# A recurrent attention block with a gated feed-forward behind it: four early inverses by halves, copies on another engine, and a new written order

## The chip, the core and the metric

The kernel runs on one core of a Trainium2 chip. A core has a matrix engine (TensorE, PE in the profile, with its weight loads as PEld), a vector engine (VectorE, DVE), a scalar engine (ScalarE, ACT), a general engine (GpSimd, POOL) and a queue that only starts transfers (SyncE, SP). Each takes its own instructions in the order in which they are written, and waits where an instruction needs what another has not delivered. Transfers (DMAs) are started by SP, by POOL and, at the very start, by ACT. The metric is the device time of one execution, in microseconds (us).

## The reference

Six arrays of shape 4 x 8 x 768 x 40 (batch, heads, steps, width) go through a recurrence with a 40 x 40 state for each of the 32 sequences:

```python
for t in range(S):
    y[:, :, t] = einsum('bhd,bhde->bhe', rt, state)
    Sa = einsum('bhde,bhe->bhd', state, at)
    state = state * wt[:, :, None, :] - einsum('bhd,bhe->bhde', Sa, bt)
    state = state + einsum('bhd,bhe->bhde', vt, kt)
```

The outputs of the 8 heads are put side by side (3072 tokens of 320 numbers), normalised by their root mean square and scaled by `rms_g`, and go through `silu(x @ w_gate) * (x @ w_val) @ w_out` with 1536 hidden columns. The weights arrive as 64-bit floats, and the kernel itself makes 32-bit floats of them.

## The kernel before

**Chunks.** The 768 steps are cut into 24 chunks of 32. Within a chunk the recurrence is written with products of matrices, which needs the inverse of one 32 x 32 unit triangular matrix for each of the 32 sequences. For chunk `c` there are three stages. `front(c)` loads the chunk and forms decays, keys and the triangular matrices: `LT` holds them, and `where(...)` copies the valid parts of products into `LT` under masks (`near` for steps 1, 2 and 3 apart inside groups of four, `msk` for the longer levels). `inverse(c)` sends `LT` through memory (`sB`) into `M`, where each of the 128 partitions holds a quarter of the rows of one sequence, and eliminates with 31 pairs of VectorE instructions (`tmp <- Yi, M` and `Yi <- Yi, tmp`); the result goes back through memory (`sY`) into `LT`. `main(c)` uses state, inverse and keys for the chunk's outputs: it forms `Xs`, then `U = inverse x Xs`, copies `U` into `VU`, updates the state `ST`, forms the scores `As` under masks `msi`, and sums five levels into `y`; then come the norm and `xg`, the scaled, turned tokens.

**Feeds.** After each pair of chunks `feed(g)` runs the feed-forward on 256 tokens: twelve slices of the hidden columns, each with products into `ps`, a silu on ScalarE (`sg`), a product on VectorE (`hT`), and products into `po`. There are 12 feeds. `narrow_slice(f)` turns the 64-bit weights into 32-bit ones on VectorE and ScalarE and writes them to memory (`sW`); this is spread over the first feed, and every feed loads its slices from `sW`.

**The order.** Nothing is scheduled while the kernel is built. Each stage only records pieces (one instruction, or one group of products), and `ORDER` is a written list that says in which order the recorded pieces are issued; `PAIRS` says which pair of PSUM banks each room uses. A piece's place in the list fixes its place in its engine's queue. A dash in the list issues a dummy product of the identity into an unused corner of `po` (`plan.warm`, line 1002 in the profile). It computes nothing. The numbers in the functions' arguments (`more=`, load names, the tables `PRODUCTS` and `LOADS`) only describe pieces to the plan; with a written list they change no instruction.

The profile gives most instructions the line of a helper: 475 for VectorE, 502, 498 and 505 for ScalarE, 521 and 524 for products, 518 for transfers, 514 for POOL's memsets. So the text goes by the names of tiles.

Of the kernel before, what the change touches and what calls it, by code (L numbers as in the profile page):

```python
# [7 lines left out]
FP32 = mybir.dt.float32  # L8
# [8 lines left out]
P = 128  # L17
# [4 lines left out]
S0, S1 = 15.0, 2.0  # L22
LEAD = 2
WARM = 230.0
# [3 lines left out]
PRODUCTS = {  # L28
    "out": (0.915, 0.359, 0.434, 0, 2560), "h": (1.618, 0.306, 0.381, 0, 4096), "h64": (0.864, 0.2, 0.2, 1, 2048),
    "turn": (0.824, 0.2, 0.273, 0, 2048), "turn3": (0.278, 0.3, 0.275, 0, 768), "turn4": (0.388, 0.249, 0.272, 0, 1024),  # L30
    "turny": (0.46, 0.145, 0.248, 2, 640), "gram": (0.927, 0.124, 0.264, 2, 512), "gramk": (0.927, 0.158, 0.263, 2, 1792),
    "score": (0.927, 0.138, 0.243, 2, 1024), "level": (0.603, 0.132, 0.216, 5, 1024), "state": (0.597, 0.126, 0.245, 3, 640),
    "lower": (0.594, 0.126, 0.216, 4, 320), "update": (0.603, 0.154, 0.265, 2, 1280), "y0": (0.613, 0.132, 0.236, 2, 1024),
}

LOADS = {
    "sB": (1.75, 0.1), "LT": (2.0, 0.2), "M": (2.67, 0.44), "sY": (1.96, 0.3), "wf": (4.02, 1.46), "r": (4.25, 0.69),
    "tok": (2.09, 0.27), "wn": (2.36, 0.31), "wan": (2.68, 0.51), "out": (1.9, 0.15), "g": (2.37, 0.68),
    "raw2": (3.1, 0.75), "raw64": (2.21, 0.27), "rawo": (2.9, 0.7), "rawp": (2.4, 0.3), "sW": (1.5, 0.7),
}  # L40
# [5 lines left out]
36 33 2 26 42 1 31 0 25 343 37 29 107 38 24 36 26 34 262 2 13 1 35 40 0 190 24 339 13 14 - - - 40 17 44 15 41 43 55  # L46
42 8 60 47 175 72 48 45 84 185 59 68 186 585 54 58 - - - - - 49 93 586 53 179 69 71 599 81 176 57 597 50 67 178 609
70 188 80 622 51 92 16 623 65 610 52 56 177 633 64 66 - - - - - - - - - - - - 61 189 9 598 77 79 187 78 587 620 62 0
587 81 - - - - 72 75 179 82 62 90 595 384 194 588 87 11 633 89 589 74 395 620 197 590 380 88 73 195 391 - - - - 101
196 209 390 610 84 102 214 381 201 611 202 5 212 86 213 383 591 85 0 222 92 591 611 17 95 221 224 223 384 94 234 225  # L50
- - 197 233 237 93 391 245 246 592 328 393 198 598 645 612 0 641 598 15 612 592 - 338 205 206 380 642 599 209 0 207
612 200 0 337 612 186 598 6 326 613 2 599 641 34 176 200 216 217 23 600 389 215 33 201 355 95 202 177 96 214 - - - -
211 187 339 93 0 577 0 561 578 297 579 171 192 53 187 191 - - - 182 188 200 623 172 185 625 186 580 562 581 612 355
582 199 1065 197 583 611 183 198 624 184 0 152 1005 850 298 0 298 0 837 295 0 0 0 83 130 298 148 0 298 83 0 507 307
833 0 303 555 0 840 307 0 290 0 67 125 316 314 0 132 125 67 0 0 131 314 0 286 325 0 130 0 298 130 0 291 292 - - - -
- 287 0 293 0 304 0 316 305 301 0 0 283 0 296 0 311 0 322 281 0 286 0 295 280 0 292 - - - - - - - - - - - - - - - -
- 288 0 0 0 0 301 0 285 62 301 116 305 0 283 250 116 0 - - - - - - - - 293 0 258 112 296 0 110 300 256 0 308 307 245
293 292 0 0 304 0 288 0 301 - - - - - - 298 306 0 0 313 0 297 0 0 0 293 310 494 301 0 494 0 302 0 0 299 492 0 0 296
0 246 0 791 0 0 0 787 0 0 93 468 2 796 94 469 0 94 462 794 0 467 93 94 290 461 95 462 96 468 511 97 469 291 98 470
481 289 99 292 471 0 99 100 101 471 102 472 103 481 511 104 482 105 488 106 489 107 483 2 490 108 109 0 293 109 490  # L60
0 108 0 0 379 0 379 387 0 387 369 0 405 378 387 406 0 - - - - - - - - - - - - - - - - - - - - - - - - - - - - - - -
- - - - - - - - - - - - - - - - - - - - - - - - - - - - - - - - - - - - - - - - 44 0 367 377 0 415 0 42 0 414 383 43
412 0 383 410 0 383 40 373 0 0 0 0 0 0 36 0 377 - - - - - - - - - - - - - - - - - 44 0 377 35 44 0 414 0 0 82 0 32 -
43 0 373 0 90 0 229 407 38 88 0 40 78 226 42 38 41 47 48 0 43 226 42 50 45 48 396 0 50 396 43 0 396 0 0 379 395 380
0 395 380 0 401 0 394 0 378 242 400 44 0 400 47 0 145 45 377 242 0 145 391 377 0 216 1 145 391 42 635 398 429 626
146 0 397 39 145 426 634 398 146 147 631 43 623 44 621 45 632 46 148 47 622 - - - - 639 375 376 149 48 416 239 641
830 150 399 377 640 840 0 150 641 653 48 838 151 658 152 645 828 - - - - - - 642 153 670 154 646 155 682 49 656 50
156 669 657 51 157 666 158 667 52 159 643 668 - - - - - - - 53 389 160 161 678 162 1 651 652 - 647 2 702 655 3 654 0
594 610 611 609 625 595 636 109 608 110 596 373 - - - - - - - - - - - 605 590 374 111 345 783 607 626 782 383 112
627 620 622 385 793 113 623 606 375 382 114 792 621 - - - - - - - 617 384 115 376 346 116 377 619 117 635 634 118  # L70
618 378 119 - - - - - 160 633 120 379 121 163 380 161 122 381 123 162 124 164 386 - - - - - - - - - 629 125 387 126
127 128 388 129 630 130 640 631 389 638 131 390 - - - - - 167 641 132 391 133 639 134 392 168 135 393 - - - - - 165
136 394 137 138 430 139 166 571 431 581 643 140 - - - 171 721 644 580 141 642 142 570 143 174 645 144 173 145 178 -
- - 182 175 146 177 147 172 150 149 179 - - - 180 148 637 176 185 732 432 186 433 0 1065 584 283 - 39 1064 36 582 38
284 638 37 40 635 583 0 17 635 480 625 567 497 40 18 624 498 41 284 568 626 42 285 499 627 43 570 286 642 636 44 500
2 706 287 45 643 897 0 493 500 501 643 287 897 656 644 648 2 45 597 907 502 649 494 0 457 860 458 0 613 0 457 611
552 0 - 596 457 621 598 0 622 0 456 595 610 853 457 622 458 634 854 0 505 - - - 500 360 765 521 361 449 531 519 764
504 532 543 362 508 363 0 500 517 543 501 4 515 363 502 364 506 419 514 365 5 366 516 367 0 367 419 368 421 369 370
420 422 44 0 370 - 430 371 44 0 3 40 0 367 426 368 369 370 504 371 37 372 373 374 375 429 376 526 525 521 377 505
522 0 338 466 390 339 397 377 9 340 391 341 392 342 430 393 398 343 480 440 400 378 439 395 387 429 396 394 403 408  # L80
388 0 403 0 342 474 700 403 578 0 700 403 342 709 490 343 0 474 7 696 405 343 709 475 403 344 0 487 706 472 0 485
695 10 343 704 404 0 404 0 4 404 37 405 0 401 31 337 481 402 45 0 474 3 337 338 41 339 402 0 42 3 0 398 705 399 471
50 335 400 898 336 703 470 401 337 37 907 338 339 402 27 480 699 908 704 340 403 341 897 479 486 701 889 343 700 584
478 890 713 714 481 899 702 719 28 706 559 900 342 712 29 560 731 30 0 531 9 0 9 683 684 17 10 0 10 454 0 450 552 10
451 0 10 672 0 672 - - - - - - - - - - - - - - - - 662 25 0 27 670 26 0 682 680 24 695 539 677 676 678 704 661 37 -
- - - 3 36 675 662 296 4 681 434 691 663 679 692 703 672 5 0 0 428 1 680 683 42 682 666 43 687 681 667 20 40 686 21
677 695 2 22 292 0 675 705 287 0 675 287 688 0 671 0 669 665 269 7 17 410 8 682 29 411 412 30 667 413 414 0 8 665 0
675 8 681 672 9 674 0 9 672 - - - - - - - - - - 481 0 9 37 483 411 0 471 0 25 5 401 6 402 403 404 471 7 39 405 473 -
- - - - - - - - - - - 16 0 0 28 8 27 397 0 397 28 0 397 0 654 462 0 5 396 36 8 397 398 37 399 14 47 462 15 0 457 10
723 44 3 11 43 458 583 644 21 12 646 582 4 13 645 461 0 571 21 13 572 458 393 22 14 394 15 466 0 391 455 19 0 372 0  # L90
16 436 0 694 28 5 27 442 6 695 371 439 7 0 696 0 451 370 435 6 760 0 745 0 428 0 741 362 425 0 751 433 362 741 0 748
362 0 425 423 358 733 0 358 0 744 358 432 359 360 0 427 428 0 7 359 0 359 15 0 359 360 6 0 425 0 428 442 359 360 361
362 363 364 0 360 361 742 362 0 362 363 364 419 365 742 366 367 2 368 423 751 369 370 371 372 373 424 675 374 7 0
424 2 0 1154 672 0 1154 421 422 732 432 738 0 669 730 1002 732 670 420 995 731 439 742 685 985 421 0 993 421 687 735
# [160 lines left out]

class Piece:


    def __init__(self, engine, key, issue, time, tail, drain=0.0, mode=-1, area=0, many=0, load=None, since=0.0):
        self.engine, self.key, self.issue = engine, key, issue  # L260
        self.time, self.tail, self.drain, self.mode, self.area = time, tail, drain, mode, area
# [773 lines left out]
```

## Time and profile before

| | |
|---|---|
| median of 3 runs | 1106.53 us (1105.67 to 1109.04) |
| the profiled execution | 1106.7 us, all of it span |
| TensorE busy | 1032.9 us, of which 75.7 in dummy products |
| VectorE busy | 907.4 us |
| ScalarE busy | 453.9 us |
| POOL busy | 302.7 us |
| first `hT` of the first feed | starts at 173.5 us |
| dummy products | from 5.3 to 225.5 us |

The profiled execution's time stands 0.2 us from the median, so its rows can be used against the median as they are. Busy time is the time covered by an engine's instructions. VectorE's and ScalarE's rows overlap: an instruction starts some 0.1 us before the row of the one in front ends, so the sum of a queue's rows is more than its busy time. "us to landing" is the time from the issue of a transfer to its end.

### The profile page before, as it was taken

How to read it: one execution, taken by the hardware profiler on the slowest of the kernel's cores; microseconds unless marked ns; L12 is line 12 of the kernel's file. 1: busy time of each engine (PE TensorE's matmuls, PEld its weight loads, DVE VectorE, ACT ScalarE, POOL GpSimd, SP SyncE). 2: the span in 40 equal slices, each digit the busy share in tenths (PEclk: the TensorE clock that was granted, in tenths of full speed). 3: DMA queues.
4: the chain of work that ended last, by engine and by line, in shares of the span. 5: the costliest groups of instructions: out<-in, count | busy, mean ns of one | idle time of the engine just before them, and what ended most of it. 6: DMA issues, size and time to landing. Idle time of an engine off the chain costs nothing.

```text
span 1106.7 us, 53122 instructions
## 1 busy us (share of the span) xinstructions
PE 1032.9 (93%) x23152; PEld 852.5 (77%) x23152; DVE 907.4 (82%) x3065; ACT 453.9 (41%) x989; POOL 302.7 (27%) x534
## 2 busy tenths in 40 slices
PE   5697888989999999999999999999989999999998
PEld 4597877767778877877777877887878878787876
DVE  5998999799889888798789789988898889798421
ACT  3644544654244344344344345334335435332211
POOL 7520342122233223223323323413404312200000
PEclk9789899989999999999999999999999999999999
DMA  7545453786555536456535545645636546434242
GB/s 158 134 85 164 122 125 85 198 240 165 124 141 124 149 80 160 117 125 141 150 101 138 138 123 134 154 101 151 139 95 166 125 112 147 108 108 131 80 141 80
DMA packets 171177, 145.43 MB, mean 131 GB/s; under 512 B 123712, under 2 KB 142080, under 8 KB 170944
## 3 DMA queue, kind: packets, MB, share of 16 engines
q1 hardware_dynamic: 152576, 119.06, 39.8%
q0 software_dynamic: 16192, 22.64, 11.0%
q8 instruction: 182, 2.98, 1.2%
q10 hardware_dynamic: 2176, 0.33, 0.2%
q14 instruction: 51, 0.42, 0.1%
HBM read 125.83 MB, written 16.12 MB: 128 GB/s over the span
## 4 chain that ended last, share of the span: by engine, by line
PE 59%; DVE 19%; issue 7%; ACT 3%; DMA 3%; POOL 2%; SPq 0%; DVEq 0%; POOLq 0%; ACTq 0%
PE ps L521 41%; PE po L521 11%; PE ps L524 7%; DVE LT L475 3%; DVE tmp L475 3%; DVE Yi L475 2%; DVE As L475 2%; DVE y L475 2%; DVE K L475 1%; DVE hT L475 1%; DVE r L475 1%; DVE ex L475 1%; DVE wf L475 1%; ACT K L502 1%; DMA sB<-LT 1%
## 5 line engine op out<-in xcount | busy, mean ns | idle before, releaser
L521 PE MATMUL ps<-xg,wf 128*128 128x256 f32 (+1 forms) x1728 | 354.5, 392 | 3.1 <-DVE xg L475 2.1
L521 PEld LDWEIGHTS ps<-xg,wf 128*128 128x128 f32 (+1 forms) x1728 | 261.3, 189 | 58.4 <-issue 14.3
L521 PE MATMUL po<-wf,hT 128*128 128x320 f32 x576 | 178.8, 444 | 3.2 <-DVE hT L475 1.8
L475 DVE TENSOR_TENSOR tmp<-Yi,M 128x60 f32<-128x60 f32 (+24 forms) x744 | 156.0, 210 | 18.1 <-DMA M<-sB 1.9
L475 DVE TENSOR_TENSOR Yi<-Yi,tmp 128x60 f32<-128x60 f32 (+24 forms) x744 | 155.3, 209 | 15.9
L518 POOL DMA_DIRECT2D VU<-in_v_dram x92 | 53.4, 587 | 356.6 <-PE ps L524 206.3
L498 ACT ACTIVATE sg<-ps 128x256 f32<-128x256 f32 x144 | 53.7, 383 | 236.4 <-PE ps L521 225.0
L521 PEld LDWEIGHTS po<-wf,hT 128*128 128x128 f32 x576 | 102.2, 190 | 39.3 <-issue 3.7
L475 DVE TENSOR_TENSOR hT<-ps,sg 128x256 f32<-128x256 f32 x144 | 59.3, 419 | 54.7 <-ACT sg L498 53.4
L475 DVE TENSOR_TENSOR K<-K,T 128x512 f32<-128x512 f32 (+1 forms) x192 | 93.4, 495 | 8.7 <-PE ps L521 3.4
L521 PEld LDWEIGHTS ps<-Ab,K 40*64 40x64 f32 x4608 | 76.6, 137 | 30.8 <-issue 9.6
L521 PE MATMUL ps<-Ab,K 40*64 40x56 f32 x4608 | 86.4, 223 | 11.5 <-DVE K L475 3.1
L502 ACT COPY K<-K 128x256 f32<-128x256 f32 (+1 forms) x168 | 71.2, 443 | 61.9 <-PE ps L521 40.6
L475 DVE TENSOR_TENSOR As<-ps,msi 128x256 f32<-128x256 f32 (+1 forms) x192 | 83.2, 481 | 10.6 <-PE ps L521 10.4
L502 ACT COPY KN<-ps 128x640 f32<-128x640 f32 x96 | 66.4, 691 | 53.4 <-PE ps L524 20.7
L521 PEld LDWEIGHTS ps<-As,KN 128*40 128x40 f32 x3072 | 67.2, 125 | 19.5 <-issue 11.7
L521 PE MATMUL ps<-As,KN 128*40 128x32 f32 x3072 | 74.5, 206 | 7.3 <-issue 4.6
L1002 PE MATMUL po<-ident 128*128 128x128 f32 x560 | 75.7, 291 | 5.3 <-ACT po L544 5.3
L1002 PEld LDWEIGHTS po<-ident 128*128 128x128 f32 x560 | 70.4, 203 | 6.7 <-POOL wan L514 5.2
L518 POOL DMA_DIRECT2D kbn<-in_b_dram x92 | 53.6, 586 | 78.5 <-PE ps L521 70.8
L518 POOL DMA_DIRECT2D wn<-in_w_dram x92 | 51.5, 566 | 85.9 <-DVE tmp L475 32.4
L518 POOL DMA_DIRECT2D kbn<-in_k_dram x92 | 53.4, 584 | 75.7 <-PE ps L521 75.0
(124 smaller groups left out, 1529.2 us busy)
## 6 DMA issues: line engine op xcount, KB each, us to landing
wf<-sW SPq DMA_DIRECT2D x144, 480.0 KB, 4.2
M<-sB SPq DMA_DIRECT2D x96, 128.0 KB, 3.9
rn<-in_r_dram SPq DMA_DIRECT2D x24, 160.0 KB, 4.3
sW<-ex SPq DMA_DIRECT2D x16, 240.0 KB, 4.0
out_dram<-o SPq DMA_DIRECT2D x48, 80.0 KB, 3.5
kbn<-in_b_dram POOLq DMA_DIRECT2D x92, 40.0 KB, 3.2
wan<-in_w_dram POOLq DMA_DIRECT2D x46, 80.0 KB, 3.9
wan<-in_a_dram POOLq DMA_DIRECT2D x46, 80.0 KB, 4.3
```

The costliest lines, as they stand in the source:

```text
L475: plan.add("DVE", time + more + each * size(o), 0.087, lambda at: fn(at(o), *m(at)), [o], aps(*args))
L498: scalar(o, [a], lambda at: nc.scalar.activation(at(o), at(a), f, **kw), aps(acc), 0.1 if f in (AF.Square, AF.Relu) else 0.0)
L502: scalar(o, [a], lambda at: nc.scalar.copy(at(o), at(a)), extra=more)
L518: plan.add(by, 0.6 if by == "POOL" else 0.45, 0.0, lambda at: queue.dma_start(out=o, in_=i), [o], [i], load=LOADS[load], since=since)
L521: return o, lhsT, rhs, lambda at: nc.tensor.matmul(at(o), lhsT, rhs, start=start, stop=stop, skip_group_check=True), 4
L524: return o, i, ident, lambda at: nc.tensor.transpose(at(o), i, ident), 2
L1002: plan.warm = lambda: nc.tensor.matmul(po_[:, 0, DM:DM + P], ident, ident, start=False, stop=False, skip_group_check=True)
```

## The change

Four things change, and the written list is a new one.

1. For chunks 0 to 3 the stage `inverse(c)` is replaced by `early_inverse(c)`. It inverts the two 16 x 16 diagonal halves of each sequence's matrix on 64 partitions (15 pairs of VectorE instructions), and gets the off-diagonal 16 x 16 block as a product of three blocks, by two groups of 32 small products with a ScalarE copy behind each. Four tiles (`B`, `Y`, `E`, `A`) are laid over the old `M` tile. The result stays in `E`, and `main(c)` reads it there, not in `LT`.
2. The three `near` copies of each front walk the same elements in another order: the eight groups innermost, not the one to three columns.
3. Copies go from VectorE to ScalarE: two of the four `VU` copies of each chunk, the two `r2` copies of each pair of chunks, the scores of the top level (one VectorE product becomes two scaled copies), and `xg` (one VectorE product becomes three scaled copies).
4. `ORDER` and `PAIRS` are new, with 224 dashes where there were 280. The tables that only described pieces go. In `state` the same products are issued in another sequence.

```diff
+    def early_inverse(c):
+        z = Z[c]
+        plan.stage = "inverse", c
+        LT = z["LT"]
+        B, Y, E, A = halves(z["M"])
+        blank(Y[:, :, 0:HC], 0.0)
+        blank(Y.rearrange("p s t -> p (s t)")[:, 0::C + 1], 1.0)
+        for i in range(HC - 1):
+            n, m = i + 1, HC - 1 - i
+            tmp = tmp_.next()[0:2 * BH, 0:n * m].rearrange("p (s t) -> p s t", s=n)
+            tt(tmp, Y[:, 0:n, i:i + 1].to_broadcast((2 * BH, n, m)), B[:, i:i + 1, i + 1:].to_broadcast((2 * BH, n, m)), MUL)
+            tt(Y[:, 0:n, i + 1:HC], Y[:, 0:n, i + 1:HC], tmp, SUB)
+        scale(Y[0:BH, :, HC:], Y[0:BH, :, 0:HC].rearrange("p s t -> p t s"), -1.0)
+        sY = sY_.next()[:, 0:3 * HC * HC].rearrange("n (s t) -> n s t", s=HC)
+        dma(sY[:, :, 0:C], Y[0:BH])
+        dma(sY[:, :, C:], Y[BH:2 * BH, :, 0:HC])
+        blank(E[:, :, 0:HC], 0.0)
+        for i, q in each_iq:
+            dma(E[top(i, 1 - q)], sY[seq(i, q)].rearrange("m s t -> s m t"))
+        ps = plan.room()
+        pe("inv", [mm(ps[...], LT[...], E[..., HC:C]) for n, i, o in by_q])
+        copy(A[:, :, 0:HC]..., ps...)
+        ps = plan.room()
+        pe("inv", [mm(ps[...], A[...], E[..., C:]) for n, i, o in by_q])
+        copy(E[:, :, HC:C]..., ps...)
+        z["IV"] = E
...
-        for m in range(4):
-            dma(M[m * BH:(m + 1) * BH].rearrange("p s t -> p (s t)"), sB, "M")
+        if c < EARLY:
+            for u in range(2):
+                dma(halves(M)[0][u * BH:(u + 1) * BH], sB...[:, u * HC:(u + 1) * HC, u * HC:(u + 1) * HC])
+        else:
+            for m in range(4):
+                dma(M[m * BH:(m + 1) * BH].rearrange("p s t -> p (s t)"), sB)
...
-            where(LT.rearrange("p n (g j) -> p n g j", j=4)[:, :, :, dist:], near[...], g4[:, :, :, at:at + m], more=0.12)
+            where(LT.rearrange("p n (g j) -> p n j g", j=4)[:, :, dist:], near[...], g4.rearrange("p n g j -> p n j g")[:, :, at:at + m])
...
-            (copy, dcopy)[q](VU[other(i, 4 * q), ...], U[other(i, 4 * q), ...], more=0.09)
+            copy(VU[other(i, 4 * q), ...], U[other(i, 4 * q), ...])
...
-            dcopy(R["r2"][half(0)], ps[half(1), :, 0])
-            dcopy(R["r2"][half(1)], ps[half(0), :, 1])
+            copy(R["r2"][half(0)], ps[half(1), :, 0])
+            copy(R["r2"][half(1)], ps[half(0), :, 1])
...
-            if G == 1 or l == 1:
-                tt(As[:, j], sc...[:, :, None, ...].to_broadcast((P, NI, 2, 16)), msi[:, j:j + 1]..., MUL)
+            if G == 1:
+                for i in range(2):
+                    scale(As[:, j, :, i], sc.rearrange("p o n t -> p (o n) t")[:, :, 16:C], msi[:, j, i, 0:1])
...
-        tt(xg[c // CG][:, :, c % CG * P:(c % CG + 1) * P], ps, gcol[:, :, None].to_broadcast((P, KT, P)), MUL)
+        for kt in range(KT):
+            scale(xg[c // CG][:, kt, c % CG * P:(c % CG + 1) * P], ps[:, kt], gcol[:, kt:kt + 1])
```

Read off the two built programs, queue by queue: on VectorE 496 instructions stand ahead of the first `hT` before, 360 after. Ahead of it stand 238 dummies before and 153 after; behind it 42 and 71.

## The prediction

> **What bounds the kernel now.** I read the page's busy times first, then its slices, then three stretches (PE, PEld, DVE, ACT and POOL busy, granted clock), then the dummy products alone, then the VectorE rows of one front.
>
> ```profile
> span 1106.7 us, 53122 instructions
> ...
> PE 1032.9 (93%) x23152; PEld 852.5 (77%) x23152; DVE 907.4 (82%) x3065; ACT 453.9 (41%) x989; POOL 302.7 (27%) x534
> ...
> PE   5697888989999999999999999999989999999998
> ...
> DVE  5998999799889888798789789988898889798421
> ...
> PEclk9789899989999999999999999999999999999999
> ```
>
> ```profile
> 0.00:225.00 225.00, 185.13 (x4176) 165.14 (x4177) 194.21 (x630) 116.13 (x232) 81.36 (x157) 0.94 0.56 135
> 225.00:1025.00 800.00, 771.57 (x18048) 627.98 (x18048) 693.12 (x2387) 323.69 (x724) 220.25 (x375) 1.00 0.53 133
> 1025.00:1107.00 82.00, 76.24 (x932) 59.33 (x930) 20.11 (x50) 14.03 (x34) 1.10 (x2) 0.99 0.34 101
> ```
>
> The same stretches, for the dummies alone (PE, PEld, clock, DMA):
>
> ```profile
> 0.00:225.00 225.00, 74.92 (x555) 69.81 (x556) 0.94 0.56 135
> 225.00:1107.00 882.00, 0.76 (x7) 0.57 (x6) 1.00 0.51 130
> ```
>
> From the timeline of VectorE, the three near copies of the first front:
>
> ```profile
> 21.69 0.73 DVE L475 COPY_PREDICATED LT<-near,ps 128x384 f32<-128x384 uint32 x1 [0.65 <-PE ps L521]
> 22.29 0.66 DVE L475 TENSOR_TENSOR Ab<-Ab,T 128x128 f32<-128x128 f32 x2
> 22.87 0.73 DVE L475 COPY_PREDICATED LT<-near,ps 128x256 f32<-128x256 uint32 x1
> 23.39 0.46 DVE L475 TENSOR_TENSOR K<-K,T 128x256 f32<-128x256 f32 x1
> 23.76 0.71 DVE L475 COPY_PREDICATED LT<-near,ps 128x128 f32<-128x128 uint32 x1
> 24.09 1.09 DVE L475 TENSOR_TENSOR K<-K,T 128x256 f32<-128x256 f32 x2
> ```
>
> TensorE's own work is 1032.9 - 75.7 = 957.2 us, so 149.5 us of the span carry none. They lie in two places. In the first 225 us it works 185.1 - 74.9 = 110.2 us and 114.8 are lost; in the 881.7 us behind, 847.0 are work and 34.7 lost. There VectorE has 107 of 800 us free. In the first 225 us it is VectorE that is full (194.2). So the kernel has a start of one quarter of a millisecond that VectorE and the round trips through memory set, and a long rest that TensorE sets. What the change is worth is read from the start; VectorE time taken out of the rest buys little.
>
> **The change part by part.** The bound of each price comes from these rows.
>
> *The inverse.* Four chunks lose 62 VectorE steps each and get 30 shorter ones. In the start such a step is followed after 0.13 us when other work stands behind it (84.67 to 84.80 in the timeline) and after 0.24 when the next step must wait for it (84.43 to 84.67). Ahead of the first `hT` (173.5 us) stand 215 inverse steps before and 99 after, so 116 fewer: between 116 x 0.13 = 15.1 and 116 x 0.24 = 27.8 us. Most neighbours there are conversions of weights and fronts, so I take 19. What is added, per chunk: a ScalarE scaling and two copies (nearest: 128x128 copies, 0.30 to 0.40), a POOL memset (0.4 for 128x384), two groups of 32 products (nearest row 32*32, 19.4 us for 768 products, so 0.8 a group): 3.0 us in a row. Fewer transfers are issued (sY 2 for 4, M 2 for 4; SP needs 0.45 to 0.60 for each), 2 us of SP's time back. On the way of each chunk that is about +1.2; two chunks are needed before the first feed, so +2.4. The transfers land in 2.7 to 3.9 us before (sB, M, sY, LT); the new ones move smaller pieces in smaller packets, and no row shows them. Bounds: 1 us less each to 3 us more each, that is -4 to +12 on the way of two chunks; I take 0, because packets of sB and LT are as small.
>
> *Waits that it adds.* `E` lies over `B` and `Y`, so its memset on POOL waits until sY has been read. Behind it on POOL stand the loads `wn` of the next front and the `VU` loads. VectorE waits for those only at `KN`, and POOL is 81 of 225 us busy, so I cost it at nothing; without that cover it costs a landing, 3 to 4 us. `M` of chunk 2 can load only when `U` of chunk 0 has been formed, since the inverse is read out of `M`; on SP the `sY` stores of chunk 1 stand right behind that load. Before, `U` of chunk 0 starts at 92.2 and inverse 2 near 112, so 20 us of cover; in the new list they stand closer.
>
> *The near copies.* From start to start they take 0.60, 0.52 and 0.33 us, 1.45 a front, whatever their 384, 256 and 128 elements. The third keeps its very pattern (128 elements, each 4 numbers on). At its pace (0.33 / 128 = 2.6 ns) the others would take 1.0 and 0.67, +0.55 a front. At the pace of the `msk` copies, which walk four or more neighbours (26.82 to 27.15 for 256), they take 0.50 and 0.33, -0.29. The third row is the nearest, since the others get its stride: +0.5, that is +2.5 ahead of the first `hT` (five fronts) and +12 over all. [...]
>
> *Copies.* Ahead of the first `hT` VectorE loses 6 `VU` copies (0.48 each), 4 `r2` (0.69), 2 `xg` (0.56) and 2 `As` (0.68), together 8.2 us. The weights' conversions are shifted by 5 steps of 0.57, 2.9. ScalarE gets, over all: `VU` 48 x 0.42 = 20, `r2` 24 x 0.63 = 15, `As` 48 x 0.40 = 19, `xg` 72 x 0.35 = 25, the early inverse 3, in all +82, from 454 to 536, half the span. In `main` four `VU` copies in a row for two beside two are +0.84, three `xg` scalings for one product +0.5: +1.4 a chunk, two chunks ahead of the first `hT`, +2.8. Behind the start this is covered by feed products; without that cover it would be 22 x 1.4 = 31 us.
>
> *The sum for the start, first way.* First `hT`: -19 + 2.4 + 2.5 - 8.2 - 2.9 + 2.8 = -22.4, so 151. But the list leaves TensorE emptier behind that point: 71 dummies for 42. One is 75.7 / 280 = 0.27 us, and dummies filled 74.9 of the 114.8 lost us, so 29 more stand for 29 x 0.27 / 0.65 = 12 us lost. Net -10.
>
> *Second way.* Dummies stand where TensorE has nothing else in the list. If they again fill 65% of what is lost, 224 of them (60.5 us) stand for 93 us lost, for 114.8: -22. To this come 256 new products of 0.025 us, 6.5 us of TensorE's work, of which I count half, since they stand where it is empty: -19.
>
> I take -16, a little nearer to the second, which holds the whole list, while the first counts only one queue.
>
> *The rest.* Of its 34.7 lost us, waits that VectorE ended (LT 3.0, As 2.2, xg 2.1, hT 1.8 and smaller) come to about 12. VectorE has some 55 us less there. At best those 12 go; at worst silus come late by the ScalarE work put ahead of them (next section). I take -1, because a written list that is new loses its own small waits.
>
> Sum: 1106.7 - 16 - 1 = 1089.7, so 1090 us; the profiled execution is 0.2 us from the median, and I leave that out.
>
> **The rivals.**
>
> *The rest gets tighter too.* The 12 us of waits on VectorE go, and the start gains what the second way gives with the new products hidden, 22: 1073. For it: VectorE's load. Against: the waits are short and spread over many causes.
>
> *The start gives the gain back.* The early inverse's round trips become the limit: +12 for packets, +4 for POOL's memset, and `M` of chunk 2 behind `U` of chunk 0. 1090 + 16 = 1106, no change. For it: the first 225 us carry transfers all through (DMA share 0.56), and it took 13 us from the end of inverse 0 to `U` and 23 us for inverse 1. Against: fewer transfers are issued.
>
> *Slower: ScalarE makes the feeds late.* Place: the 144 silus, each waiting in ScalarE's queue behind copies that were VectorE's. Price: 0.42 us for each silu that stands behind one, if `hT` and the products of `po` then wait. It decides from 17 / 0.42 = 40 silus; at 90 of 144 it is +38, 1128. For it: `hT` waits 53.4 us for `sg` already. Against: ScalarE itself waits 225.0 us for TensorE before silus, and has 476 of 800 us free in the middle stretch.
>
> *The clock.* From 25 to 150 us it is granted at 0.78 to 0.93; with 56 dummies fewer it may be lower. The work there is 52 us; at half the clock the pieces on the way, some 10 us, would take 8 more: 1098, still faster.
>
> **How the numbers follow.** Forecast 0.56 (its own range 1078 to 1102), tighter rest 0.17, given back 0.10, late silus 0.13, clock 0.04. The range 1068 to 1112 holds all of the forecast and the clock case, three quarters of the tighter one and most of the given-back one, and leaves the late silus out: 0.8. No change means within 0.3%, 1103 to 1110, about what a measurement of this kernel can tell. Faster: 0.56 + 0.17 + 0.04 and a little of given back (0.01) less 0.01 for the forecast's own tail, 0.77; same 0.06, from given back; slower 0.17: the late silus and the rest of given back.
>
> **What would show it.** First `hT` at 145 to 157 us; dummies 60 to 61 us; VectorE 815 to 840 us busy, ScalarE 525 to 545; lost time behind the start 30 to 38 us; near copies above 0.73 us for 384 elements, 0.34 from start to start for 128. The prediction is wrong if the first `hT` is not earlier, or if the wait of `hT` for `sg` is far above 53 us.

## The result: 4.5% slower

| | |
|---|---|
| before, median on the same chip | 1106.28 us (1105.67 to 1109.04) |
| after, median of 4 executions | 1169.26 us (1153.12 to 1178.88) |
| ratio | 1.045, 95% interval 1.039 to 1.051 |
| forecast | 1090 us, range 1068 to 1112 |

The forecast was wrong in size and in sign. The ratio is that of the executions of 1153.1 and 1161.9 us (their mean, 1157.5, is what comparisons below use); the other two, of 1176.6 and 1178.9 us, ran in a slower state at a granted clock of 0.94 for 0.95 and 0.96, and the profiled one is the former, so up to 19 us of what its rows lose are its own.

The page of the kernel after, in the lines that the prediction showed of before (busy times, then the span in 40 slices):

```profile
span 1174.8 us, 53837 instructions
...
PE 1071.3 (91%) x23552; PEld 881.1 (75%) x23552; DVE 850.7 (72%) x2817; ACT 520.8 (44%) x1189; POOL 309.6 (26%) x554
...
PE   5987888988889998999999999999999899999998
...
DVE  7896877678888888675797786687876777873421
...
PEclk7798888788999999999999999899999999999999
```

VectorE did become freer (850.7 us for 907.4), and behind the first three slices it is in none fuller than TensorE. The row to look at is PEclk: it is below 9 in nine of the first ten slices, and once more in the second half. The three stretches (busy time of PE, PEld, DVE, ACT, POOL, then granted clock, DMA share, GB/s):

```profile
0.00:225.00 225.00, 185.41 (x4464) 165.57 (x4468) 173.34 (x513) 122.25 (x257) 87.67 (x177) 0.81 0.51 119
225.00:1025.00 800.00, 744.38 (x16778) 603.06 (x16767) 619.03 (x2109) 356.07 (x829) 217.40 (x369) 0.96 0.51 126
1025.00:1175.00 150.00, 141.52 (x2332) 112.49 (x2330) 58.34 (x197) 42.48 (x105) 4.52 (x8) 0.99 0.36 106
```

In the first 225 us TensorE was as busy as before, but at a clock of 0.81 for 0.94. In the middle stretch it was busy for 27 us less (744.38 for 771.57) and at 0.96 for 1.00. So the rest, which the forecast had left alone, is where time was lost.

To compare kernels I use one account, worked out from each trace. In the traces the granted clock stands at 1.0 or 0.5, in pieces of 3.4 us or a multiple of it. Real products (all but the dummies), with those at 0.5 counted half, come to 949 to 958 us in every kernel here: that is the work. Whatever a stretch has beyond its share of this work is lost there, to idle time, to dummies or to the half clock.

| lost, us (profiled executions) | 0 to 150 | 150 to 350 | behind 350 | sum |
|---|---|---|---|---|
| before | 100.9 | 28.2 | 26.0 | 155.1 |
| after | 92.3 | 69.5 | 61.8 | 223.6 |

The start gained 9 us. From 150 to 350 us 41 were lost, and behind that 36.

### The profile page after: what moved, and what is told of

It is laid out like the page before. It is cut to its first block, busy times and chain, and to the rows that moved or that the text cites. A ratio compares the mean times of both kernels' runs of the same rounds, so it can differ in the third digit from the quotient of the medians.

```text
span 1174.8 us, 53837 instructions
## 1 busy us (share of the span) xinstructions
PE 1071.3 (91%) x23552; PEld 881.1 (75%) x23552; DVE 850.7 (72%) x2817; ACT 520.8 (44%) x1189; POOL 309.6 (26%) x554
## 3 DMA queue, kind: packets, MB, share of 16 engines
q1 hardware_dynamic: 153856, 116.96, 37.1%
## 4 chain that ended last, share of the span: by engine, by line
PE 64%; DVE 15%; issue 8%; DMA 5%; ACT 4%; SPq 2%; POOL 1%; DVEq 0%; ACTq 0%; POOLq 0%
PE ps L497 42%; PE po L497 11%; PE ps L500 9%; DVE LT L455 5%; PE po L1029 2%; SPq L494 2%; DVE K L455 2%; DVE tmp L455 2%; DVE Yi L455 1%; DVE hT L455 1%; DMA wf<-in_moe_w_gate_dram 1%; DMA M<-sB 1%; DMA sB<-LT 1%; DVE Ab L455 1%; DMA kbn<-in_b_dram 1%
## 5 line engine op out<-in xcount | busy, mean ns | idle before, releaser
L497 PE MATMUL ps<-xg,wf 128*128 128x256 f32 (+1 forms) x1728 | 369.1, 404 | 6.9 <-ACT x L481 2.7
L497 PEld LDWEIGHTS ps<-xg,wf 128*128 128x128 f32 (+1 forms) x1728 | 269.7, 196 | 68.1 <-issue 20.3
L497 PE MATMUL po<-wf,hT 128*128 128x320 f32 x576 | 186.5, 455 | 1.1 <-DVE hT L455 1.0
L455 DVE TENSOR_TENSOR tmp<-Yi,M 128x60 f32<-128x60 f32 (+24 forms) x620 | 131.4, 212 | 29.6 <-DMA M<-sB 16.1
L455 DVE TENSOR_TENSOR Yi<-Yi,tmp 128x60 f32<-128x60 f32 (+24 forms) x620 | 131.5, 212 | 14.0
L497 PE MATMUL ps<-Ab,K 40*64 40x56 f32 x4608 | 93.5, 235 | 25.7 <-DVE K L455 9.0
L497 PEld LDWEIGHTS ps<-Ab,K 40*64 40x64 f32 x4608 | 83.2, 148 | 43.3 <-issue 9.5
L455 DVE COPY_PREDICATED LT<-near,ps 128x384 f32<-128x384 uint32 (+2 forms) x72 | 93.0, 1292 | 4.2 <-PE ps L497 3.9
L455 DVE TENSOR_TENSOR As<-ps,msi 128x256 f32<-128x256 f32 (+1 forms) x168 | 68.3, 455 | 22.5 <-PE ps L497 15.5
L1029 PE MATMUL po<-ident 128*128 128x128 f32 x448 | 71.2, 315 | 7.7 <-ACT po L518 5.3
```

The lines of the kernel that those rows point to most:

```text
L455: plan.add("DVE", kind, lambda at: fn(at(o), *m(at)), [o], aps(*args))
L497: return o, lhsT, rhs, lambda at: nc.tensor.matmul(at(o), lhsT, rhs, start=start, stop=stop, skip_group_check=True)
L1029: plan.warm = lambda: nc.tensor.matmul(po_[:, 0, DM:DM + P], ident, ident, start=False, stop=False, skip_group_check=True)
```

## The experiments

### The near copies alone, and all but them

One kernel is the changed one with the three `near` copies walked as before, the other the one before with only these copies walked in the new way.

```diff
-  where(LT...("p n (g j) -> p n j g")[:, :, dist:], near..., g4.rearrange("p n g j -> p n j g")[:, :, at:at + m])
+  where(LT...("p n (g j) -> p n g j")[:, :, :, dist:], near..., g4[:, :, :, at:at + m])
```

> The changed kernel with the near copies in their old element order, all else as changed. Theory N (the near copies cost it: 2.74 us a front from start to start for 1.47, the list counts on short ones, TensorE runs dry and its clock is halved): under 1100 us, near copies 0.72 us each again, granted clock 0.98. Theory O (the new list and the copies moved to ScalarE cost it, whatever the near copies take): 1130 us or more, clock under 0.97.

> The kernel before with the near copies in the new element order, and nothing else. Theory N: VectorE gets 1.28 us a front, 31 us in all, and the old list was not written for it either: slower by 15 to 40 us, 1120 to 1145. Theory O: the rest has 107 of 800 us of VectorE free, so only the first six fronts count: 1106 to 1114.

With the copies put back, the changed kernel took 1118.2 us (ratio to before 1.011, 1.004 to 1.018). Alone in the kernel before, they took it to 1161.0 (1.050, 1.047 to 1.053). So they cost about 39 us in the new list (from 1157.5) and 55 in the old one. Neither theory had these times: the copies alone cost more than theory N allowed, and putting them back did not bring the changed kernel under 1100 us. Theory O for the second run was the prediction's own argument, that VectorE's free time behind the start covers the copies; 1161 us refutes it. The number of TensorE's instructions is the same within each pair. The groups of VectorE's instructions by shape, after:

```profile
L455 DVE COPY_PREDICATED LT<-near,ps 128x384 f32<-128x384 uint32 x24 | 44.8, 1868 | 3.9 <-PE ps L497 3.9
L455 DVE COPY_PREDICATED LT<-near,ps 128x256 f32<-128x256 uint32 x24 | 30.9, 1286 | 0.1
L455 DVE COPY_PREDICATED LT<-near,ps 128x128 f32<-128x128 uint32 x24 | 17.3, 721 | 0.1
```

and before (busy us, mean ns of one, idle time ahead of it):

```profile
L475 DVE COPY_PREDICATED LT<-near,ps 128x384 f32<-128x384 uint32 x24 | 17.4, 726 | 1.2 <-PE ps L521 0.8 <-issue 0.3
L475 DVE COPY_PREDICATED LT<-near,ps 128x256 f32<-128x256 uint32 x24 | 17.4, 725 | 0.3
L475 DVE COPY_PREDICATED LT<-near,ps 128x128 f32<-128x128 uint32 x24 | 17.3, 722 | 0.4
```

Before, the three copies take 726, 725 and 722 ns for 384, 256 and 128 elements; what they share is the 128 groups, of three, two and one neighbours, that each walks. After, every element is a step of its own: 384, 256 and 128 steps take 1868, 1286 and 721 ns, (1868 - 721) / 256 = 4.5 ns a step. From start to start a front's three copies take 1.49 + 0.91 + 0.34 = 2.74 us for 1.46, that is +1.28 us a front and 31 us of VectorE over 24 fronts.

31 us on VectorE became 39 and 55 on the span. Those who waited for these copies, in the kernel before (first two lines of the answer for the tile: waiter, us, times) and in the one with the new walk alone:

```profile
  PEld ps L521: 5.6, 6
  PE ps L521: 3.4, 5
```

```profile
  PE ps L521: 20.4, 12
  PEld ps L521: 19.7, 10
```

In the account the kernel with the new walk alone has 29 us more idle time of TensorE and 25 us more lost to the half clock (91.6 us at half for 37.4). So in this account the idle time is little more than half of the loss.

### The copies

In these two the `VU`, `r2`, top-level score and `xg` copies of the changed kernel go back to VectorE at their places in the new list, with the near copies new and old.

```diff
-  copy(VU[other(i, 4 * q), ...], U...)
+  (copy, dcopy)[q](VU[other(i, 4 * q), ...], U...)
-  copy(R["r2"]...)                        # both halves
+  dcopy(R["r2"]...)
-  scale(As[:, j, :, i], ..., msi[:, j, i, 0:1])
+  tt(As[:, j, :, i], ..., msi[:, j:j + 1, i].to_broadcast((P, NI, 16)), MUL)
-  scale(xg[...], ps[:, kt], gcol[:, kt:kt + 1])
+  tt(xg[...], ps[:, kt], gcol[:, kt:kt + 1].to_broadcast((P, P)), MUL)
```

> The changed kernel with its copies (VU, r2, top-level scores, xg) on VectorE again, in the same places of the list; the top-level scores and xg stay two and three instructions. Theory N: VectorE gets some 75 us more beside the long near copies: slower than the changed kernel by 10 us or more. Theory O: if ScalarE's longer queue is what makes hT late, it is faster than the changed kernel by 20 us or more, and hT's wait for sg falls from 106 us towards 53.

> The changed kernel with both undone, so only the early inverse and the new list are left. Theory N: between 1080 and 1115 us, no better than with the near copies alone put back. Theory O: faster than with the near copies alone put back by 10 us or more.

1192.4 us for 1157.5, and 1150.5 for 1118.2: the move to ScalarE is worth 35 and 32 us in the new list. (For the second run both theories were off: 1080 to 1115 us, or faster than 1118.2.) So the rival by which ScalarE's new work makes the feeds late is out as a cost on balance. `hT` does wait twice as long for `sg` as before, in the kernel after and in the one with the near copies back alike. But it waits nearly as long with the copies on VectorE again (88.2 and 94.7 us), and the same in two kernels 39 us apart, so this wait, which the prediction named as the sign of failure, says little. Before, after, and with the near copies back:

```profile
DVE hT L475 <- ACT sg L498: 53.4, 35, 7.9
```

```profile
DVE hT L455 <- ACT sg L475: 105.9, 53, 8.7
```

```profile
DVE hT L455 <- ACT sg L475: 105.2, 53, 8.7
```

The next two make the same move in the list of before, all four copies and then only `VU` and `r2`, at the places of the instructions that they replace.

The diff is the one above read upward (for the second only its first two pairs); these kernels, and all later ones with parts of the change in the old list, also keep the changed kernel's sequence of products in `state` and eight small copies of the identity into `M` on POOL at the start.

> The kernel before, its own list with all 280 dashes, with the copies of VU, r2, the top level's scores and xg moved to ScalarE at the places of the old instructions, and nothing else of the change. Theory K (VectorE is the late one everywhere, as moving the same copies back cost 23 and 32 us under the new list): VectorE's busy time falls by 70 to 85 us and the kernel takes 1085 to 1100 us. Rival (the old list was written for VectorE's copies, and ScalarE comes to them late, behind silus and turns): 1105 to 1125 us, with more idle time of TensorE ended by ScalarE's VU, r2, As or xg.

> The kernel before, its own list, with only the VU and r2 copies on ScalarE; the top level's scores and xg stay one VectorE product each. With all four moved TensorE waited 8.2 us behind the start for xg from ScalarE and VectorE 26.9 us for ScalarE's part of the scores. Theory X (it is these two that cost the 16 us): 1096 to 1107 us. Rival V (the VU and r2 copies come late on ScalarE too, U to state being the chain that sets each chunk): 1110 to 1122 us.

All four: 1125.0 us, ratio 1.015 (1.009 to 1.021). `VU` and `r2` alone: 1103.1 us, 0.998 (0.996 to 1.000). With all four, TensorE's and VectorE's waits behind 250 us show the other two (us, times, longest; before, TensorE waits 2.1 us for VectorE's `xg`, and VectorE for no ScalarE scores):

```profile
PE ps L510 <- ACT xg L494: 8.2, 11, 2.0
```

```profile
DVE As L468 <- ACT As L494: 26.9, 29, 4.0
```

So a place written for VectorE's copy seems too late for three ScalarE copies of `xg`. What a move between engines is worth depends on the list: 32 to 35 us gained in one, 16 lost in the other.

### What is left: 1118 for 1106

With the near copies back the first 150 us lose 24.5 us less than before (76.4 for 100.9), about as forecast, and 150 to 350 us lose 22.6 more (50.8 for 28.2). Two explanations were tried first. One was the half clock: 93.5 us of it for 37.4. So dummies were added where TensorE was idle, first in this kernel, then in the first 250 us of the one before; and all dummies were taken out of the one before.

```diff
-... 68 - - 63 554 ...
+... 68 - - - - - - - - - - - 63 554 ...     (123 more, at 41 places)
-... - - - 40 17 44 15 ...
+... - - - - - - - - - - 40 17 - - - - - - - - - - - - - - 44 15 ...     (90 more, at 25 places)
-... 13 14 - - - 40 17 44 ...
+... 13 14 40 17 44 ...     (all 280 out)
```

> The changed kernel with the near copies in their old order (1118.2 us) and 123 more dashes in its list: at every place where its trace shows TensorE idle for more than 0.45 us (41 places, 46.5 us), as many dummy products as fill four fifths of the gap at 0.3 us each. Nothing else is changed. Theory C (the clock): of the 13.4 us by which the profiled execution of the kernel with near copies back was longer than the one before, 22 are real products made slower by the halved clock (66.5 us of them ran at half against 22.0 before; at full clock the real products take 954 and 952 us). Filling the gaps keeps the clock up: half clock under 50 us instead of 93, and 1098 to 1110 us. Theory F (the new list holds the start back by itself: narrowing ends 31 us later, chunks run ahead of feeds): the dummies take the place of idle time and nothing more, 1115 to 1125 us.

> The kernel before with 90 more dashes in its list, at the 25 places of the first 250 us where its trace shows TensorE idle for more than 0.45 us (34 us), four fifths of each gap at 0.3 us a dummy. Theory C (of the kernel before 22 us of real products ran at half clock, 11 us lost): half clock under 15 us instead of 37, and 1096 to 1103 us. Rival F (the start is paced by VectorE and the round trips; as with the changed kernel's gaps, dummies only take the place of idle time): 1104 to 1112 us.

> The kernel before with all 280 dashes taken out of its list, so that no dummy product runs; all else is the same. Theory C (the clock): gaps in the first 226 us halve the clock for well over 100 us instead of 37, real products there run at half speed: 1112 to 1140 us. Rival (dummies only stand in idle time, the start is bound by VectorE and round trips whatever the clock): within 4 us of the kernel before, or a few us faster, as no real product waits behind a dummy.

The first came to 1120.0 us: the clock was back (37.2 us at half) and the time was not. The second took 1137.3 us, ratio 1.028 (1.024 to 1.032), and the third 1157.5, 1.044 (1.038 to 1.051). The last two don't fit the account of the clock, nor its rival: up to 350 us the second lost less than the kernel before (125.4 for 129.1), and the third only 8 more. Both lost their time behind 350 us, 54.4 and 58.2 for 26.0, where their lists are the very same as that of the kernel before.

The other explanation was that the early inverse and the copies don't pay at all. So the early inverse was put into the list of before, alone and with all copies. Its steps stand at the places of the old inverse's first 15 pairs, its products ahead of `U`, and 65 of the 71 dashes ahead of the first `U` are out.

```diff
+  (early_inverse if c + 2 < EARLY else inverse)(c + 2)
-  inverse(c + 2)
```

> The kernel before with the early inverse by halves for chunks 0 to 3 and nothing else of the change: its pieces stand at the places of the old inverse's first 15 steps, the two groups of small products directly ahead of U, and 65 of the 71 dashes that stood ahead of the first U are taken out, as U comes earlier. Theory S (the start is set by VectorE and the round trips, as the prediction had it): first U at 78 to 84 instead of 92 us, first hT at 150 to 162 instead of 173.5, and 1088 to 1101 us. Rival G (the start's gain is given back: fewer dummies and more gaps halve the clock, or M of chunk 2, which now waits for the first U, is the next to be late): first hT at 160 to 173 and 1102 to 1118 us.

> The kernel before with the early inverse (as it stood alone under the old list, 1123.3 us) and all the moved copies (alone 1125.0 us) together, near copies in the old order: the same pieces as the changed kernel with the near copies put back (1118.2 us), but in the old list. Theory A (the two costs add, and the new list is what makes up for part of them): 1130 to 1146 us, so that the new list is worth 12 to 28 us for these pieces. Rival J (the parts need each other: only a VectorE relieved of copies can use the early start): 1100 to 1118 us, and the new list is worth nothing or harms.

1123.3 us (1.014, 1.009 to 1.018) and 1135.2 (1.025, 1.021 to 1.029): 15 for the early inverse and 16 for the copies make 30 together, the first more than either theory had. With the same pieces the new list takes 1118.2, so it is worth 17 us. At the places that I gave it the early inverse gains only 3 us in the first 150 (97.8 for 100.9): the first `U` starts at 86.7 us for 92.2, but the first `hT` at 177.4, 4 us later than before, and from 75 to 240 us VectorE waits 13.5 us for ScalarE's `VU` copies, for 1.0. The 24 us come only with the new list.

### The blocks of TensorE's instructions

In the trace of the kernel with the near copies back, many of TensorE's idle pieces lie in the middle of a group of products that waits for nothing. They come at a distance of 127.2 records or a multiple. (The records hold each product twice, each time with a weight load, so that 280 dummies are 560 records; the counts here are of records.) The page has a queue that fits this (packets, MB, share), in the kernel before:

```profile
q8 instruction: 182, 2.98, 1.2%
```

These are 182 transfers of 16,384 bytes. I take them to bring TensorE's own instructions, by their number: 23,152 products and as many weight loads are 46,304 instructions, 254.4 of them or 127.2 products for a transfer, which is the period; with all 280 dummies out, 1,120 instructions fewer, the page has 177 transfers. Below, a block is what one transfer brings. 2.98 MB for 46,304 are 64.4 bytes for each; at 64, as an estimate, a block is 256 instructions, a few of them not among the records. Of the idle pieces over 0.25 us, 20 in the kernel before (15.2 us) end 1.2 to 1.75 us after the landing of such a block; were the landings 2 us earlier or later, it would be 4 or 3 (2.4 or 1.5 us). (At 4 us earlier it is 16 again, because the next block often lands 3.4 to 4.2 us behind.) With the near copies back it is 30 pieces and 31.2 us, and 29 of the 30 stand within 6 records of one place in the period of 127.2; in the kernel after it is 36 and 37.7 us. I call them block waits. The two stretched kernels had them too: 29.2 us with 90 more dummies, 30.2 with none.

So the stream was shifted and nothing else. Narrow dummies were put in the list at the start, where TensorE idles for 5 us (3.4 in the changed kernel).

```diff
+  plan.fill = lambda: nc.tensor.matmul(po_[:, 0, DM:DM + 16], ident, ident[:, 0:16], start=False, stop=False, ...)
...
-... - - - 40 17 44 15 ...
+... - - - 40 17 . . . . . . . . . . . . . . . . 44 15 ...     (a dot issues plan.fill)
```

> The kernel before with 16 narrow dummy products (identity by 16 of its columns) ahead of its second group of turns, where TensorE is idle for 5 us. They do no work that the rest waits for; they only shift all later products by 32 records in TensorE's stream of instructions, a quarter of the 127 records that one transfer of 16 KB of instructions brings. Theory I (TensorE waits at the ends of such blocks, and which products stand there decides how long): the idle time that ends 1.2 to 1.75 us after the landing of a block, 15.2 us in the kernel before (8.1 behind 250 us), becomes another by 5 us or more, and the time goes the same way by one to two times as much: outside 1102 to 1110 us, longer more likely than shorter. Rival N (what was seen at the blocks' ends is hidden or chance): 1103 to 1109 us.

> The same with 32 narrow dummies, half a block. Theory I: as with 16, another sum of idle time behind the landings than 15.2 us and a time that follows it; over this run and the one with 16 at least one lies more than 6 us from the kernel before. Rival N: 1103 to 1110 us.

> The changed kernel with the near copies put back (1118.2 us; 31.2 us of idle time behind the landings of instruction blocks, 16.0 of it behind 250 us), shifted by half a block with 32 narrow dummies ahead of its first products of decays, where TensorE is idle for 3.4 us. Theory I: the idle time at the blocks' ends changes by 8 us or more, more likely downward as 31 is much, and the time follows: 1098 to 1112 us, or over 1124. Rival L (the rest of the loss is the list's: VectorE has waits among the narrowing from 150 to 350 us): 1114 to 1122 us whatever the shift.

> The same as the run before with 48 narrow dummies, three quarters of a block. Theory I: another sum at the blocks' ends and a time that follows it by one to two times; between the shifts of 0, 32 and 48 the times lie more than 8 us apart. Rival L: 1114 to 1123 us.

The kernel before went to 1136.4 us with 16 dummies (1.028, 1.024 to 1.031) and to 1166.8 with 32 (1.056, 1.052 to 1.060); the changed one with near copies back to 1131.5 and 1140.2. Block waits went to 29.3, 37.1, 38.4 and 37.0 us. The first `hT` came 8.2 us later with the 32 in the kernel before, and not later with the 16, so most of it is lost behind. But the dummies take time of their own (6.8 us for the 16, 13.7 for the 32), and more dummies had cost more. A whole block tells the two apart. The next dummies are 16 by 16, and 32 of them take 1.9 us, 64 take 3.6; by the records each is two products and two weight loads, four instructions, so 32 are half a block of 256 and 64 a whole one.

```diff
+  plan.fill = lambda: nc.tensor.matmul(po_[0:16, 0, DM:DM + 16], ident[0:16, 0:16], ident[0:16, 0:16], start=False, stop=False, ...)
```

> The kernel before with 32 tiny dummy products (16 by 16) ahead of its second group of turns, where TensorE is idle for 5 us: 128 instructions of 64 bytes, half of a 16 KB block, and under 2 us of TensorE's time. Theory I (the place of the blocks' ends): as long as the run shifted by 32 narrow dummies was behind its first hT, 1140 to 1160 us, with over 20 us of idle time behind landings after 250 us (8.1 before). Rival R (dummies at this place harm by their own time or by what they displace): with a sixth of the time of the narrow ones, 1104 to 1120 us.

> The same with 64 tiny dummies: 256 instructions, one whole block. Theory I: all later products stand to the blocks' ends as in the kernel before, so nearly nothing is lost: 1102 to 1114 us, under 12 us of idle time behind landings after 250 us. Rival R (the more dummies, the worse): not shorter than the run with 32.

Half a block: 1153.5 us, ratio 1.045 (1.041 to 1.048). A whole block: 1104.9 us, 1.000 (0.998 to 1.002). With twice the dummies the loss is gone, so it is not their time or their number but the place of the blocks' ends. TensorE's timeline shows one wait, with half a block (start, us, instruction, records, and the idle time ahead of it with what ended it):

```profile
335.13 1.16 PE L541 MATMUL ps<-Ab,K 40*64 40x56 f32 x64
336.31 1.00 PE L541 MATMUL ps<-rE,vut 40*64 40x32 f32 x52
339.56 0.64 PE L541 MATMUL ps<-rE,vut 40*64 40x32 f32 x12 [2.25 <-issue]
```

and the same products with a whole block:

```profile
329.49 1.15 PE L542 MATMUL ps<-Ab,K 40*64 40x56 f32 x64
330.66 1.14 PE L542 MATMUL ps<-rE,vut 40*64 40x32 f32 x64
331.94 3.06 PE L542 MATMUL ps<-xg,wf 64*128 64x256 f32 x16
```

The group of 64 stops after 52 for 2.25 us; by the trace the block had landed 1.33 us before it goes on. Behind it the 16 products `ps<-xg,wf` take 5.8 us (340.1 to 345.9) for 3.06, at a granted clock of 0.5 from 339.1 to 346.0. In the list of what TensorE waited for behind 250 us (us, times, longest) such waits are part of "issue", which the prediction passed over because it names nobody. Before, with half a block, and with a whole one:

```profile
PE ps L521 <- issue: 5.5, 12, 1.3
```

```profile
PE ps L541 <- issue: 26.7, 26, 2.3
```

```profile
PE ps L542 <- issue: 5.3, 10, 0.8
```

Behind 250 us the block waits are 8.1 us in the kernel before and 26.1 us with half a block, which takes 48 us longer.

The last run uses the shift: `VU` and `r2` on ScalarE, shifted by two tiny dummies.

```diff
-... - - 48 17 18 19 ...
+... - - 48 17 . . 18 19 ...
```

> The kernel before with only the VU and r2 copies on ScalarE (1103.1 us), shifted by two tiny dummies, 8 instructions. From the pace of its products by its own trace the ends of the blocks then stand a little better: theory I gives 1096 to 1102 us, faster than both kernels; if the shift is too small to matter, 1101 to 1105 us.

1100.3 us, ratio 0.995 (0.993 to 0.997): faster than both kernels, by 0.5% of the one before. It is within the noise of the same kernel without the two dummies (1103.1 us, 11.5 us of block waits; 11.7 here), so the shift is not shown to add anything; and for the copies alone the interval reaches 1.000.

| | median us | half clock us | block waits us | lost to 150 | 150 to 350 | behind 350 |
|---|---|---|---|---|---|---|
| before | 1106 | 37 | 15.2 | 100.9 | 28.2 | 26.0 |
| after (rows: the execution of 1177 us) | 1157 | 147 | 37.7 | 92.3 | 69.5 | 61.8 |
| after, near copies back | 1118 | 94 | 31.2 | 76.4 | 50.8 | 38.8 |
| before, near copies new | 1161 | 92 | 11.2 | 103.4 | 37.7 | 69.3 |
| before, all copies moved | 1125 | 45 | 9.7 | 99.2 | 29.4 | 40.9 |
| before, early inverse | 1123 | 82 | 14.7 | 97.8 | 40.3 | 27.7 |
| before, early inverse and all copies | 1135 | 87 | 13.6 | 98.6 | 41.9 | 41.4 |
| before, 16 narrow dummies | 1136 | 79 | 29.3 | 100.7 | 31.4 | 53.7 |
| before, half a block | 1154 | 99 | 32.3 | 101.0 | 40.2 | 62.4 |
| before, a whole block | 1105 | 45 | 13.1 | 100.7 | 28.2 | 25.3 |

## Why the prediction was wrong, step by step

Of the 67 us between the forecast and 1157.5, the near copies are 39, which is shown. The other 28 are lost behind 150 us, where the prediction had the rest at -1; why is in part argued.

**The near copies: the term that was mis-sized.** I took +0.5 us a front; it is +1.28. I read the pace of a single step from the third copy as 0.33 us from start to start over 128 elements, 2.6 ns. But a part of that copy's 0.72 us ran under the next instruction, and what the rows said was that three copies of 128 groups take the same time, 0.73 us, so that the price is by the step from group to group. By it the first copy has 256 steps more and the second 128, 1.14 and 0.56 us on their rows; from start to start it is 0.91 and 0.38. That price is shown for groups of one to three neighbours. The `msk` copies, 256 elements in 64 runs of 4, 32 of 8 and 16 of 16 neighbours, take 0.43, 0.43 and 0.44 us, so with these longer runs the time does not follow their number.

**Where that term lies.** I put 2.5 us of it into the sum, for the five fronts ahead of the first `hT`, and left the other 19 fronts out, because VectorE has 107 of 800 us free behind the start. That was the larger error. The copies write `LT`, for which a front's next products wait, and free time elsewhere doesn't cover that. "VectorE time taken out of the rest buys little" had been true; time put in cost 1.3 times itself in the new list and 1.8 times in the old one.

**The start.** The sum of -22 for the first `hT` was right for the changed list, or a little short: with the near copies back, the first `U` starts at 80 us for 92, the first `hT` at 146 for 173.5 (forecast 151), and 24 us less are lost by 150 us. That the inverse's -19 is the term which made it is not shown, since alone in the old list the early inverse left the first `hT` 4 us later. With the near copies in, the first `hT` is at 164 in the profiled execution: 18 us for five fronts whose copies take 6.4 us more.

**Second way, and dummies.** 71.2 us of dummies, not 60.5: 224 of them at 0.318 us, mostly, as I estimate, because the clock of the first 225 us is lower than in the rows from which I took 0.27 (0.81 for 0.94, and 0.27 x 0.94 / 0.81 is 0.31). That dummies fill a fixed share of what is lost was a poor rule; taking all of them out cost 8 us up to 350 us.

**The rest, -1.** In the profiled execution it lost 36 us behind 350 us and 41 between 150 and 350; with the near copies back 13 and 23 are left of that. No step had a stretch in which the start's gain is spent: with the near copies back, 150 to 350 us take back 22.6 of the 24.5 us. VectorE is less busy there than before, though its weight conversions now run on past 250 us (8.0 us of work on `wf` there for 0.4). From 150 to 250 us (PE, PEld, DVE, ACT, POOL, clock), before and with the near copies back:

```profile
150.00:250.00 100.00, 88.56 (x2179) 73.89 (x2180) 90.53 (x278) 55.55 (x108) 29.53 (x50) 0.97 0.61 162
```

```profile
150.00:250.00 100.00, 87.57 (x2156) 74.27 (x2155) 77.58 (x265) 51.94 (x113) 26.85 (x43) 0.86 0.54 144
```

TensorE is as busy, at a clock of 0.86 for 0.97. From 150 to 350 us the block waits are 11.0 us for 3.0, and 27 us run at half clock for 7.

**What no step had: the instruction blocks.** The change alters the number of TensorE's instructions (23,552 products in the records for 23,152: 512 more in the early chunks' two groups, 112 fewer of dummies, and a weight load with each), so all later products stand elsewhere to the blocks' ends. A shift by half a block alone made the kernel before 4.5% slower. How much of the changed kernel's time this is was not isolated: shifting its whole stream by a half and three quarters of a block made it worse, with 38.4 and 37.0 us of block waits, and with their narrow dummies these two lose 3 and 9 us more ahead of 150 us. As an estimate from the five shift runs in which block waits rose, a us of them comes with 1.8 us (near copies back, half a block: 13.3 / 7.2) to 3.8 us (the same, three quarters: 22.0 / 5.8) of time, so its 16 us more would be worth 29 to 61, enough to hide what the start gained. That is argued, not shown, and other runs speak against so simple a price. With 123 more dummies the block waits fell to 25.8 us and the time stayed at 1120; and in the old list the early inverse, alone and with all copies, has only 14.7 and 13.6 us of block waits and is still 15 and 30 us slower than before. VectorE's waits in the new list are a rival that no run tests: from 150 to 250 us it waits 6.2 us for `sg` and 5.5 for ScalarE's `wf`, for 1.1 and 0.3 before.

**The rivals.** *Start gives the gain back* had the right outcome for the kernel with the near copies back and the wrong place: not the round trips ahead of the first `hT`, but the 200 us behind it. *Late silus* is out as a cost of the moved copies on balance. *The clock* does fall, and by more than its 8 us: real products at half clock cost 22 us more than before with the near copies back (66.5 us of them for 22.0) and 45 in the profiled execution after (112.4). But with the near copies back 44 of these 66.5 us stand behind 150 us (5 before), not in the start that the rival named, and where dummies brought the clock back the time stayed. *Rest tighter* is out.

**Copies.** VectorE at 850.7 us was forecast at 815 to 840; with the near copies at 31 us and not 12 it would have been 834 to 859. ScalarE at 520.8 is 4 below the range.

## What to carry to other kernels

Where rows of different sizes take the same time, ask what number they do share, and price the edit by that number. An engine with free time in a stretch is no cover for an instruction that somebody waits for there. And before a change of TensorE's instructions is judged in a long kernel of small products, shift the stream by a fraction of a block and by a whole one: here the same work ran from 1105 to 1154 us by that alone, and a change tuned at one place of the blocks is compared with another at a worse one.

## What was not expected of the hardware

TensorE's instructions seem to come in blocks: the kernel before has 182 transfers of 16,384 bytes for 46,304 instructions, 254.4 for each or 127.2 products, and with the near copies back the idle pieces come at that distance. A run of small products, 64 in 1.15 us, takes 2.3 us for 127 of them, and over all these kernels the next transfer starts under 2.3 us after the landing of the one before in only 5 of some 3,650 cases (1.9 at the earliest; 2.36 in the kernel before). A transfer mostly takes 0.9 to 1.4 us (at most 2.8), so that blocks land hardly ever less than 3.3 us apart (17 times, 2.9 at the least; 3.34 in the kernel before), and where products stop at a block's end they mostly go on 1.2 to 1.75 us behind a landing. So I take such a run to reach the end of its block before the next is there. With half a block the granted clock fell to 0.5 for 6.8 us during an idle piece of 2.25 us, and 16 products took 5.8 us and not 3.06. The near copies took 0.15 us and 4.5 ns for each step between groups, whether a group has one element or three.
